# A gated mix of linear attention and eight experts on one core: the queries' sums by head move from TensorE to ScalarE and VectorE, a Silu moves behind a copy, and tiles are resized

## The chip, the cores and the metric

The kernel runs on one core of a Trainium2 chip. The core has five engines with a queue of instructions each: TensorE (PE in the profile, with its weight loads as PEld), VectorE (DVE), ScalarE (ACT), GpSimd (POOL) and SyncE (SP). Each engine takes its instructions strictly in the order in which the program emits them, and waits on semaphores where an operand isn't ready or a buffer isn't free. SP, POOL and ACT also issue DMAs. The metric is the device time of one execution in microseconds; lower is better.

## The reference

`x` has 2048 rows (tokens) of 512. Two branches are computed from it and mixed row by row:

```
qkv = x @ wqkv                                  # 32 heads of 16
phi(t) = where(t > 0, t + 1, exp(t)) + 1e-6;    pq, pk = phi(q), phi(k)
kv  = sum_s pk v^T   (per head, 16 x 16);       z = sum_s pk   (per head, 16)
o   = (pq kv) / (pq . z + 1e-6);                a = o @ wo
b   = sum_e  softmax(x @ w_gate)_e * (silu(x @ w1[e]) @ w2[e])     # all 8 experts, F = 1792
out = g * a + (1 - g) * b,    g = sigmoid(x . gate_w)
```

The divisor `pq . z` is the "sum by head" of the title: for each token and each of the 32 heads, a sum over the head's 16 features of `phi(q) * z`.

## The kernel before

**Number format.** Every fp32 operand of a large product is split into a high part in TensorE's fast fp32 format and a low remainder, and a product is three matmuls (`mm3`, lines 60 to 62: high by high, high by low, low by high). The high part is a ScalarE copy (`act_copy`, line 65), the low part a VectorE subtraction.

**Stages.** `keys` (the first 103 us) loads x, computes phi(k), the router's logits and the gate's (`g_proj`, matmuls of line 459, two passes of 256 and 266 columns from the weights `gw`), and accumulates `ys` = phi(k) with x over 16 blocks of 128 tokens (`y_acc`: moving operand `pkh`, stationary operand `xt`). For the first 12 blocks `xt` lies in the pool `w1p`, for the last four in the pool `att`; `pkh` always lies in `att`. `pks` sums phi(k) by DMA. Then `experts` runs one long loop over the step `u`. The branch b and the branch a use the same machinery: the attention is the ninth "expert", whose first weights are wq and whose second weights are wo folded with kv.

**The loop.** The first layer goes by groups `g` (a pair of 128-feature blocks of one expert, for one half of the tokens), and a group takes seven steps `k` = 0 to 6 of `up`, one product of six matmuls each, in a seven-product scheme on 2 x 2 blocks. The products share four PSUM banks: two under the tag "a", one "b", one "c". ScalarE and VectorE read a bank between two products that accumulate in it, so TensorE waits where such a read is late. In step 3 `hidden(g, 0, 0, ...)` applies Silu to bank b; in step 4 `act_copy(sn[g, 2], bank a)` copies bank a, which product 5 of step 6 goes on accumulating in; step 5 adds bank c on VectorE (line 698), step 6 adds bank a on VectorE (line 704), and product 6 (step 1 of the next group, `a<-t6h` in the early groups) accumulates in that bank once more.
From step u = 58 on, each step also holds a tick `n = u - 58` of the second layer (`tick`, six matmuls `p<-ho,w`), with results taken out of PSUM in `evict`. A step with its tick lasts some 2.7 us. `other()` emits the preparatory work of a step ahead of its matmuls: weights of the next groups (`prep`), high and low parts of the hidden values (`high`, `low_h`), block differences (`differ`) and the queries.
The order of groups is: the two of the attention for half 0, the experts of half 0, four experts of half 1, the attention for half 1, the other four experts. So the first expert's first group is g = 2, and its first Silu (step u = 17) is the first use of that function; a table load on ScalarE stands ahead of it in the trace.

**The queries.** phi(q) is written to DRAM (`pqd`) in four pieces i = 0 to 3 of 512 features by 512 tokens. While the parts of `m.beside` (experts 0, 1, 4 and 5 of half 1) run, one piece each is loaded (at s = -3, s being the tick within the part), gets the constant 1e-6, is divided by its heads' sums and multiplied by the gate g, and is written back:

- `queries_first`, s = 0 to 3: `act_copy(..., bias=EPS)` on ScalarE, one of the four feature blocks each tick
- `queries_last`, s = 3: four products `Q.z` by `Q.d` on TensorE (line 1040, 32 columns of weights, plain fp32, which the trace shows as 8 matmul records), into a bank of tag "a"
- s = 4: a ScalarE copy of that bank to `r`; SP loads the gate, broadcast to 128 partitions
- s = 5 to 8: four reciprocals of 128 columns; s = 9: the product with the gate, and four POOL DMAs to DRAM (`rd`)
- s = 10 and 15: POOL DMAs read `rd` back so that a head's value stands on its 16 partitions (line 1006); s = 15 to 18: four VectorE products (line 1030) and the write to `pqd`

`normaliser` makes `Q.z` at u = 7: z by 32 tiny matmul records (line 943) against `ones`, masked with `maskh` on VectorE, and parked in DRAM (`zcd`).

**The end.** The last part is the attention of half 1, two groups (`A[1]`). In its product P5, `evict` adds the banks to the sums already loaded (`sums`, tile `tl`, line 843), two VectorE adds for each `sub`; then `columns(2)` and `turn_last` transpose some of the sums on TensorE (lines 1083, 1104), and `last_rows` accumulates the last product onto them.

**Tile addresses.** All tiles of the pools `xpool`, `w1p`, `hq` and `w2p` have sizes that are multiples of 256 bytes for each partition, and lie 128 bytes past a multiple of 256. In `att`, the second weight tile g1 has 8576 bytes (33 and a half times 256), so what comes after it in that pool (the raw x tiles, `hl` and `xe` with `pkh` and the split x) lies at a multiple of 256.

Of the kernel before, what the change touches and what calls it, by code (L numbers as in the profile page):

```python
# [16 lines left out]
P = 128  # L17
# [3 lines left out]
E = 8  # L21
# [23 lines left out]
def gated_mix_kernel(ctx: ExitStack, tc: tile.TileContext, xT, x, wk, wv, wqkv_q, wo, wm, out):  # L45
# [59 lines left out]
    m.zcd = dram.tile([P, KT * NH], F32, name="zcd")  # L105
    m.rd = dram.tile([2, 2, NH, TB], F32, name="rd")

# [218 lines left out]
def keys(m):  # L326
# [34 lines left out]
    maskh = m.maskh = misc.tile([P, KT, NH], F32, name="maskh")  # L361
# [33 lines left out]
    v.memset(f32(zero), 0.0)  # L395
# [52 lines left out]
    def bands(t):  # L448
        if t == 5:
            band(mask.rearrange("p (b e) -> p b e", e=DH), [[-DH, P // DH], [0, DH]], 1)  # L450
        elif t == 6:
            band(maskh, [[P, KT], [-DH, NH]], 1)

    pk = {}

# [130 lines left out]
def experts(m, misc):  # L586
# [58 lines left out]
    def touch():  # L645
        b = ps_tile("b", "b")
        o, at = ops[0][0]
        nc.tensor.matmul(b, o[:, 0, at:at + P], XO[0][0][0][:, 0], start=True, stop=True)

    def up(g, k, mid, other):
        old = g > 0
        new = g < NG
        if k == 0:
            other()
            if old:
                hidden(g - 1, 1, 1, sn[g - 1, 3], sn[g - 1, 3])
            if new:
                bank[g, "a"] = ps_tile(f"a{g}", "a")  # L660
                product(g, 0, bank[g, "a"], True)
            mid()
            if new:

                bank[g, "b"] = ps_tile(f"b{g}", "b")
                act_copy(bank[g, "b"], bank[g, "a"])
        elif k == 1:
            other()
            if old:
                product(g - 1, 6, bank[g - 1, "a"], False)  # L670
            mid()
            if old:
                hidden(g - 1, 1, 0, r_tile(f"s4_{g - 1}"), bank[g - 1, "a"])
        elif k == 2:
            other()
            if new:
                bank[g, "c"] = ps_tile(f"c{g}", "c")
                product(g, 1, bank[g, "c"], True)
            mid()
            if new:  # L680
                sn[g, 3] = r_tile(f"s3_{g}")
                act_copy(sn[g, 3], bank[g, "c"])
        elif k == 3:
            other()
            product(g, 2, bank[g, "b"], False)
            mid()
            hidden(g, 0, 0, r_tile(f"s1_{g}"), bank[g, "b"])
        elif k == 4:
            other()
            product(g, 3, bank[g, "a"], False)  # L690
            mid()
            sn[g, 2] = r_tile(f"s2_{g}")
            act_copy(sn[g, 2], bank[g, "a"])
        elif k == 5:
            other()
            product(g, 4, bank[g, "c"], False)
            mid()
            v.tensor_add(sn[g, 2], bank[g, "c"], sn[g, 2])  # L698
        else:
            other()  # L700
            hidden(g, 0, 1, sn[g, 2], sn[g, 2])
            product(g, 5, bank[g, "a"], False)
            mid()
            v.tensor_add(sn[g, 3], bank[g, "a"], sn[g, 3])  # L704
# [125 lines left out]
    def evict(part, prod, sub):  # L830
        b = pb[bank_of(part, prod), sub]
        e = f"{part.h}_{part.e}{sub}"

        own = part is m.parts[-2]
        if part is m.A[1]:

            if prod == "P1":
                own_bank(sub)
                return

            for r, j in {"P7": [(1, 1)], "P2": [(0, 0)], "P4": [(1, 0)], "P6": [(1, 0)], "P5": [(0, 1), (1, 1)]}[prod]:
                s = sums[1, r * 2 + sub, j]
                v.tensor_add(s, b, s)
# [93 lines left out]


    def normaliser():
        ps = ps_tile("z", "dn")[:, :KT * NH]  # L940
        for c in range(KT):
            for a in range(QT):
                nc.tensor.matmul(ps[a * SQ:(a + 1) * SQ, c * NH:(c + 1) * NH],
                                 m.pks[:, c * P + a * SQ:c * P + (a + 1) * SQ], m.ones, start=(c == 0), stop=True,
                                 skip_group_check=True)
        zf = r_tile("zf")[:, :KT * NH].rearrange("p (c f) -> p c f", c=KT)
        v.scalar_tensor_tensor(zf, ps.rearrange("p (c f) -> p c f", c=KT), S * EPS, m.maskh, op0=ALU.add, op1=ALU.mult)
        nc.sync.dma_start(m.zcd, zf.rearrange("p c f -> p (c f)"))

    def gates(step):  # L950
        g = m.lg[:, :, :E]
# [36 lines left out]

    Q = SimpleNamespace()

    def queries_load(i):
        if i % 2 == 0:
            az = m.raw_tile(f"az{i}")
            Q.z = az[:, :KT * NH].rearrange("p (c f) -> p c f", c=KT)
            Q.by = [az[:, KT * NH + c * TB:KT * NH + (c + 1) * TB] for c in (0, 1, 2, 0)]
            nc.sync.dma_start(az[:, :KT * NH], m.zcd)
# [4 lines left out]
    def queries_first(i, s):  # L1001
        h, j = divmod(i, 2)

        def spread(c):
            heads = m.rd[h, j, c * P // DH:(c + 1) * P // DH]
            nc.gpsimd.dma_start(Q.by[c], heads[:, None, :].to_broadcast([P // DH, DH, TB]))

        if 0 <= s < KT:
            act_copy(Q.d[:, s], Q.d[:, s], bias=EPS)
        elif s == 4:  # L1010
            r = Q.r = out_tile(f"r{i}")
            Q.gate = out_tile(f"rg{i}")
            at = (2 * h + j) * TB
            nc.sync.dma_start(Q.gate, m.wgtd[E:E + 1, at:at + TB].to_broadcast([P, TB]))
            act_copy(r, Q.ps, bias=EPS)
        if 5 <= s < 9:
            r = Q.r[:, (s - 5) * P:(s - 4) * P]
            v.reciprocal(r, r)
        elif s == 9:
            v.tensor_mul(Q.r, Q.r, Q.gate)  # L1020
            for c in range(KT):
                n = P // DH
                at = c * (NH + n)
                nc.gpsimd.dma_start(m.rd[h, j, c * n:(c + 1) * n], Q.r[at:at + n])
        elif s == 10:
            for c in range(KT - 1):
                spread(c)
        if 15 <= s < 15 + KT:
            d = Q.d[:, s - 15]
            v.tensor_mul(d, d, Q.by[s - 15])  # L1030
            nc.sync.dma_start(m.pqd[h, j, s - 15], d)
            if s == 15:
                spread(KT - 1)

    def queries_last(i, s):

        if s == KT - 1:
            Q.ps = ps_tile(f"dn{i}", "a")
            for c in range(KT):
                nc.tensor.matmul(Q.ps[c * NH:(c + 1) * NH, :], Q.z[:, c], Q.d[:, c], start=True, stop=True)  # L1040


    def load_query(part, i):
# [104 lines left out]
    for u in range(LAG + NTICK):  # L1148
# [2 lines left out]
        g, k = divmod(u, 7)  # L1151


        query = [(i, n - part.t0) for i, part in enumerate(m.beside) if -3 <= n - part.t0 < 20]

        def mid():
            if n >= 0:
                tick(n)
            for i, s in query:
                queries_last(i, s)  # L1160


        def spare(i, name):
# [7 lines left out]
        def other():  # L1171
# [16 lines left out]
            for i, s in query:  # L1188
                if s == -3:
                    queries_load(i)  # L1190
                queries_first(i, s)
            q, s = divmod(u - 7 * WP, 21)
            if 0 <= q < 2 and s == 0:
                m.load_wp(q)
# [100 lines left out]
```

## Time and profile before

| | us |
|---|---|
| median of 3 runs | 2328.27 (2327.76, 2328.27, 2330.57) |
| profiled execution | 2327.1 |
| its span, first to last instruction | 2325.1 |
| TensorE busy | 2317.9 |
| VectorE busy | 1808.4 |
| ScalarE busy | 1400.4 |
| GpSimd busy | 171.2 |

The granted TensorE clock is full throughout. A line of the page's groups names the line of the kernel, the engine, the operation, the tile written and the tiles read, then the count, the busy time in us and the mean duration in ns. In a timeline a row is the start in us, the duration in us, the engine, the line and the tiles. Matmuls are pipelined, so one that shows 0.39 us lets the next start 0.23 us later: a cost on TensorE is read from start to start, not from durations.

### The profile page before, as it was taken

How to read it: one execution, taken by the hardware profiler on the slowest of the kernel's cores; microseconds unless marked ns; L12 is line 12 of the kernel's file. 1: busy time of each engine (PE TensorE's matmuls, PEld its weight loads, DVE VectorE, ACT ScalarE, POOL GpSimd, SP SyncE). 2: the span in 40 equal slices, each digit the busy share in tenths (PEclk: the TensorE clock that was granted, in tenths of full speed). 3: DMA queues.
4: the chain of work that ended last, by engine and by line, in shares of the span. 5: the costliest groups of instructions: out<-in, count | busy, mean ns of one | idle time of the engine just before them, and what ended most of it. 6: DMA issues, size and time to landing. Idle time of an engine off the chain costs nothing.

```text
span 2325.1 us, 31697 instructions
## 1 busy us (share of the span) xinstructions
PE 2317.9 (100%) x10582; PEld 1919.7 (83%) x10582; DVE 1808.4 (78%) x3088; ACT 1400.4 (60%) x2641; POOL 171.2 (7%) x241
## 2 busy tenths in 40 slices
PE   9999999999999999999999999999999999999999
PEld 8888888888888888888888888888888888888887
DVE  6798888888888878888677768776777776777777
ACT  6687656666666666666555555555565555555553
POOL 1101000000000000000001001000011100100101
PEclk9999999999999999999999999999999999999999
DMA  7898888988889798888846556665556646666568
GB/s 233 235 305 293 269 278 255 286 261 264 266 271 282 250 290 259 264 271 258 290 138 178 166 182 172 178 187 143 162 174 181 201 152 185 182 164 175 161 220 223
DMA packets 325620, 517.54 MB, mean 223 GB/s; under 512 B 51328, under 2 KB 220560, under 8 KB 325072
## 3 DMA queue, kind: packets, MB, share of 16 engines
q1 hardware_dynamic: 294720, 463.91, 60.5%
q0 software_dynamic: 26080, 50.69, 11.9%
q8 instruction: 83, 1.36, 0.2%
q10 hardware_dynamic: 4656, 0.92, 0.2%
q14 instruction: 81, 0.66, 0.1%
HBM read 347.75 MB, written 163.45 MB: 220 GB/s over the span
## 4 chain that ended last, share of the span: by engine, by line
PE 99%; ACT 0%; issue 0%; DVE 0%
PE p L60 16%; PE p L62 16%; PE p L61 16%; PE a L60 9%; PE a L61 9%; PE a L62 9%; PE c L60 4%; PE c L62 4%; PE c L61 4%; PE b L60 2%; PE b L62 2%; PE b L61 2%; PE g L459 2%; PE y L60 1%; PE y L62 1%; PE y L61 1%
## 5 line engine op out<-in xcount | busy, mean ns | idle before, releaser
L60 PE MATMUL p<-ho,w 128*128 128x512 f32 x1602 | 623.2, 389 | 0.0
L61 PE MATMUL p<-ho,w 128*128 128x512 f32 x1602 | 623.2, 389 | 0.0
L62 PE MATMUL p<-ho,w 128*128 128x512 f32 x1602 | 623.2, 389 | 0.0
L768 DVE TENSOR_TENSOR ho<-s,ho 128x512 fp32r<-128x512 f32 x784 | 536.7, 685 | 41.0 <-ACT ho L65 38.3
L65 ACT ACTIVATE ho<-s 128x512 fp32r<-128x512 f32 x784 | 481.4, 621 | 16.0 <-PE p L62 10.8
L62 PEld LDWEIGHTS p<-ho,w 128*128 128x128 f32 x1602 | 300.6, 188 | 62.7
L60 PEld LDWEIGHTS p<-ho,w 128*128 128x128 f32 x1602 | 300.7, 188 | 62.3
L61 PEld LDWEIGHTS p<-ho,w 128*128 128x128 f32 x1602 | 300.7, 188 | 62.3
L65 ACT ACTIVATE o<-rs 128x512 fp32r<-128x512 f32 x224 | 129.2, 577 | 205.7 <-PE c L62 114.0
L65 ACT ACTIVATE o<-rm 128x512 fp32r<-128x512 f32 x240 | 138.4, 577 | 142.1 <-PE a L62 68.4
L698 DVE TENSOR_TENSOR s<-c,s 128x512 f32<-128x512 f32 x116 | 80.1, 690 | 156.9 <-PE c L62 150.6
L65 ACT ACTIVATE ws<-rm 128x256 fp32r<-128x256 f32 (+1 forms) x204 | 115.0, 572 | 53.1 <-DMA w2stash<-ws 48.7
L627 ACT ACTIVATE s<-s 128x512 f32<-128x512 f32 x224 | 138.4, 618 | 6.2 <-DVE s L704 3.7
L704 DVE TENSOR_TENSOR s<-a,s 128x512 f32<-128x512 f32 x116 | 80.1, 690 | 63.2 <-PE a L62 63.2
L627 ACT ACTIVATE s<-b 128x512 f32<-128x512 f32 x112 | 67.0, 598 | 102.9 <-PE b L62 91.0
L65 ACT ACTIVATE s<-a 128x512 f32<-128x512 f32 x116 | 69.3, 597 | 92.1 <-PE a L62 92.1
L207 DVE TENSOR_TENSOR o<-rm,o 128x512 fp32r<-128x512 f32 x180 | 123.0, 683 | 1.3 <-ACT o L65 1.2
L221 DVE TENSOR_TENSOR ws<-rm,ws 128x512 fp32r<-128x512 f32 x155 | 106.1, 685 | 21.2 <-ACT ws L65 19.4
L207 DVE TENSOR_TENSOR o<-rs,o 128x512 fp32r<-128x512 f32 x168 | 114.5, 682 | 8.5 <-ACT o L65 8.5
L65 ACT ACTIVATE b<-a 128x512 f32<-128x512 f32 x116 | 67.2, 579 | 64.2 <-PE a L62 64.2
L65 ACT ACTIVATE s<-c 128x512 f32<-128x512 f32 x116 | 69.0, 595 | 26.3 <-PE c L62 26.3
L827 POOL DMA_DIRECT2D acct<-c x30 | 26.3, 876 | 693.0 <-DVE c L821 526.4
(331 smaller groups left out, 4521.1 us busy)
## 6 DMA issues: line engine op xcount, KB each, us to landing
w<-w2stash SPq DMA_DIRECT2D x403, 512.0 KB, 4.2
w2stash<-ws SPq DMA_DIRECT2D x359, 256.0 KB, 4.6
rm<-wm SPq DMA_DIRECT2D x228, 256.0 KB, 5.2
rs<-wm SPq DMA_DIRECT2D x108, 256.0 KB, 4.2
wb<-wgtd SPq DMA_DIRECT2D x16, 512.0 KB, 4.8
acct<-c POOLq DMA_DIRECT2D x30, 256.0 KB, 6.2
acct<-d POOLq DMA_DIRECT2D x30, 256.0 KB, 5.2
acct<-k POOLq DMA_DIRECT2D x30, 256.0 KB, 5.3
```

The source lines that it names most:

```text
L60: nc.tensor.matmul(ps, wh, xh, start=start, stop=False, skip_group_check=True)
L61: nc.tensor.matmul(ps, wh, xl, start=False, stop=False, skip_group_check=True)
L62: nc.tensor.matmul(ps, wlo, xh, start=False, stop=stop, skip_group_check=True)
L65: nc.scalar.activation(dst, src, AF.Copy, scale=scale, bias=bias)
L207: v.tensor_sub(two(o, 1), src, f32(two(o, 0)))
L221: v.tensor_sub(two(w, 1), src, f32(two(w, 0)))
L459: nc.tensor.matmul(ps, xk((0, 0, 1)[j], tb, k, tt * P, (tt + 1) * P), gw[g][:, (0, 1, 0)[j], k, :], start=(k == 0 and j == 0), stop=(k == ...
L627: nc.scalar.activation(dst, src, AF.Silu)
L698: v.tensor_add(sn[g, 2], bank[g, "c"], sn[g, 2])
L704: v.tensor_add(sn[g, 3], bank[g, "a"], sn[g, 3])
L768: v.tensor_sub(h[1], s, f32(h[0]))
L827: nc.gpsimd.dma_start(m.acct[part.h, j, dt], s, accum_op=ALU.add)
```

## The change

1. **Sums by head.** The four small products on TensorE are gone, with the DRAM round trips `zcd` and `rd`. `normaliser` now uses two columns of `ones` instead of 32 and keeps z, one value for each feature, in a small SBUF tile `m.z`; `maskh` is gone. For each piece, over 22 ticks instead of 19: for each of the four feature blocks c, ScalarE adds 1e-6 as before and writes a second copy scaled by `m.z` (a value per partition); VectorE transposes that copy in squares of 32 and, a tick later, reduces groups of 16 columns to a head's sum. Then one addition and one reciprocal of 128 columns (s = 12), one product with the gate (s = 13), and for each c a transpose whose input repeats each value 16 times (back to features on partitions) and, a tick later, the product with the block and its write. The gate is loaded by four POOL DMAs at s = -3, as 32 x 16 elements of 4 bytes each.
2. **Phase.** g1 takes 320 columns for each row block instead of 266 (10240 bytes), so the tiles of `att` after it lie 128 bytes past a multiple of 256, like those of the other pools.
3. **First Silu.** For group EXP0 (g = 2) alone, `hidden(g, 0, 0, ...)` is emitted in step 4 behind the copy of bank a, instead of in step 3.
4. **End.** In P5 of the last part, `sub` 0 adds its two sums in the other order.

```diff
+    EXP0 = m.parts[0].gs[0]
...
-            hidden(g, 0, 0, r_tile(f"s1_{g}"), bank[g, "b"])
+            if g != EXP0:
+                hidden(g, 0, 0, r_tile(f"s1_{g}"), bank[g, "b"])
         elif k == 4:
...
             act_copy(sn[g, 2], bank[g, "a"])
+            if g == EXP0:
+                hidden(g, 0, 0, r_tile(f"s1_{g}"), bank[g, "b"])
...
-    gw = [att.tile([P, 2048 + 96 * i], F32R, name=f"g{i}")[:, :2 * KT * G[i]] for i in range(2)]
-    gw = [g.rearrange("p (c k f) -> p c k f", c=2, k=KT) for g in gw]
+    gw = [att.tile([P, 2 * KT * w], F32R, name=f"g{i}") for i, w in enumerate((256, 320))]
+    gw = [g.rearrange("p (c k f) -> p c k f", c=2, k=KT)[:, :, :, :n] for g, n in zip(gw, G)]
...
+            last = [(1, 1), (0, 1)][::1 - 2 * sub]
+            for r, j in {"P7": [(1, 1)], "P2": [(0, 0)], "P4": [(1, 0)], "P6": [(1, 0)], "P5": last}[prod]:
...
+    QS = 3 * KT + 2 + 2 * KT
...
+            *Q.t, Q.sq, rest = (az[:, c * TB:(c + 1) * TB] for c in range(KT))
+            Q.r, Q.gate = rest[:, :P], rest[:, P:P + TB // SQ]
...
+        gate = m.wgtd[E, i * TB:(i + 1) * TB].rearrange("(b i) -> i b", i=SQ)
+        for a in range(QT):
+            nc.gpsimd.dma_start(Q.gate[a * SQ:(a + 1) * SQ], gate)
+
+    def queries(i, s):
...
+        if 0 <= s < 3 * KT:
+            c, step = divmod(s, 3)
+            if step == 0:
+                act_copy(Q.d[:, c], Q.d[:, c], bias=EPS)
+                nc.scalar.activation(Q.t[c % 2], Q.d[:, c], AF.Copy, scale=m.z[:, c:c + 1])
+            elif step == 1:
+                v.transpose(Q.sq, Q.t[c % 2])
+            else:
+                v.tensor_reduce(heads(c), Q.sq.rearrange("p (n f) -> p n f", f=DH), axis=AX.X, op=ALU.add)
+        elif s == 3 * KT:
+            v.tensor_scalar(Q.r, Q.r, EPS, None, op0=ALU.add)
+            v.reciprocal(Q.r, Q.r)
+        elif s == 3 * KT + 1:
+            r = Q.r.rearrange("p (c b h) -> p c b h", c=KT, h=SQ // DH)
+            v.tensor_mul(r, r, Q.gate[:, None, :, None].to_broadcast([P, KT, TB // SQ, SQ // DH]))
+        elif s < QS:
+            c, step = divmod(s - 3 * KT - 2, 2)
+            if step == 0:
+                v.transpose(Q.t[c % 2], heads(c)[:, :, None].to_broadcast([P, SQ, DH]))
+            else:
+                d = Q.d[:, c]
+                v.tensor_mul(d, d, Q.t[c % 2])
+                nc.sync.dma_start(m.pqd[h, j, c], d)
```

More of the change, by code (lines that the diff above doesn't have):

```diff
@@ L104, in gated_mix_kernel @@
     m.wpd = [dram.tile([P, D], F32, name=f"wpd{c}") for c in range(KT)]
-    m.zcd = dram.tile([P, KT * NH], F32, name="zcd")
-    m.rd = dram.tile([2, 2, NH, TB], F32, name="rd")
     X = [[SimpleNamespace(e=e, h=h, n=NPAIR) for e in range(E)] for h in range(2)]
@@ L360, in keys @@
     mask = m.mask = misc.tile([P, P], F32, name="mask")
-    maskh = m.maskh = misc.tile([P, KT, NH], F32, name="maskh")
     pks = m.pks = misc.tile([P, D], F32, name="pks")
@@ L450, in bands @@
             band(mask.rearrange("p (b e) -> p b e", e=DH), [[-DH, P // DH], [0, DH]], 1)
-        elif t == 6:
-            band(maskh, [[P, KT], [-DH, NH]], 1)
     pk = {}
@@ L839, in evict @@
                 return
-            for r, j in {"P7": [(1, 1)], "P2": [(0, 0)], "P4": [(1, 0)], "P6": [(1, 0)], "P5": [(0, 1), (1, 1)]}[prod]:
+            last = [(1, 1), (0, 1)][::1 - 2 * sub]
+            for r, j in {"P7": [(1, 1)], "P2": [(0, 0)], "P4": [(1, 0)], "P6": [(1, 0)], "P5": last}[prod]:
                 s = sums[1, r * 2 + sub, j]
@@ L939, in normaliser @@
     def normaliser():
-        ps = ps_tile("z", "dn")[:, :KT * NH]
+        ps = ps_tile("z", "dn")[:, :2 * KT]
         for c in range(KT):
             for a in range(QT):
[L943 to L948, printed above, removed]
+                nc.tensor.matmul(ps[a * SQ:(a + 1) * SQ, 2 * c:2 * c + 2],
+                                 m.pks[:, c * P + a * SQ:c * P + (a + 1) * SQ], m.ones[:, :2], start=(c == 0),
+                                 stop=True, skip_group_check=True)
+        m.z = hp.tile([P, 2 * SQ], F32, name="z", tag="z", bufs=1)
+        v.tensor_scalar(m.z[:, :KT], ps.rearrange("p (c f) -> p c f", f=2)[:, :, 0], S * EPS, None, op0=ALU.add)
     def gates(step):
@@ L993, in queries_load @@
             az = m.raw_tile(f"az{i}")
-            Q.z = az[:, :KT * NH].rearrange("p (c f) -> p c f", c=KT)
-            Q.by = [az[:, KT * NH + c * TB:KT * NH + (c + 1) * TB] for c in (0, 1, 2, 0)]
-            nc.sync.dma_start(az[:, :KT * NH], m.zcd)
+            *Q.t, Q.sq, rest = (az[:, c * TB:(c + 1) * TB] for c in range(KT))
+            Q.r, Q.gate = rest[:, :P], rest[:, P:P + TB // SQ]
         Q.d = m.raw_tile(f"pq{i}").rearrange("p (c t) -> p c t", c=KT)
@@ L999, in queries_load @@
             nc.sync.dma_start(Q.d[:, c], m.pqd[i // 2, i % 2, c])
-    def queries_first(i, s):
+        gate = m.wgtd[E, i * TB:(i + 1) * TB].rearrange("(b i) -> i b", i=SQ)
+        for a in range(QT):
+            nc.gpsimd.dma_start(Q.gate[a * SQ:(a + 1) * SQ], gate)
+    def queries(i, s):
         h, j = divmod(i, 2)
[L1004 to L1040, printed above, removed]
+        def heads(c):
+            return Q.r[:, c * SQ:(c + 1) * SQ]
+        if 0 <= s < 3 * KT:
[21 more added lines that the diff above has]
+                nc.sync.dma_start(m.pqd[h, j, c], d)
@@ L1151, in experts @@
         g, k = divmod(u, 7)
-        query = [(i, n - part.t0) for i, part in enumerate(m.beside) if -3 <= n - part.t0 < 20]
+        query = [(i, n - part.t0) for i, part in enumerate(m.beside) if -3 <= n - part.t0 < QS]
         def mid():
@@ L1158, in mid @@
                 tick(n)
-            for i, s in query:
-                queries_last(i, s)
         def spare(i, name):
@@ L1190, in other @@
                     queries_load(i)
-                queries_first(i, s)
+                if s >= 0:
+                    queries(i, s)
             q, s = divmod(u - 7 * WP, 21)
```

## The prediction

> **What bounds the kernel now.** I read, in this order: the page's busy times and chain, TensorE's own waits, then timelines around the places that the change touches.
>
> ```profile
> span 2325.1 us, 31697 instructions
> ...
> PE 2317.9 (100%) x10582; PEld 1919.7 (83%) x10582; DVE 1808.4 (78%) x3088; ACT 1400.4 (60%) x2641; POOL 171.2 (7%) x241
> ...
> PE 99%; ACT 0%; issue 0%; DVE 0%
> ```
>
> ```profile
> PE idle L523 <- DVE zero L395: 1.5, 1, 1.5
> PE a L60 <- ACT s L65: 0.7, 1, 0.7
> ```
>
> TensorE is the chain from end to end, and in the whole span it waits by name twice. So what leaves TensorE's queue leaves the time one for one, and added work on VectorE or ScalarE costs nothing until it makes TensorE wait. All that counts below is measured on TensorE from start to start.
>
> **Sums by head off TensorE: -6.6 us.** The first of the four places:
>
> ```profile
> 1256.73 0.39 PE L62 MATMUL p<-ho,w 128*128 128x512 f32 x1
> 1257.05 1.52 PE L1040 MATMUL dn<-pq,az 128*32 128x512 f32 x8
> 1258.50 0.50 PE L60 MATMUL a<-n5h,o 128*128 128x512 f32 x1
> 1258.83 0.40 PE L61 MATMUL a<-n5l,o 128*128 128x512 f32 x1
> ...
> L1040 PE MATMUL dn<-pq,az x32: 592/605/617, 1257.0 to 1967.5; 128*32 128x512 f32 x32
> ```
>
> From the start of the last ordinary matmul ahead (1256.73) to that of the second behind (1258.83) pass 2.10 us; without the eight records it would be two ordinary steps of 0.227 (from the last pair of the rows on phase, below), 0.45. That is 1.65 us a piece, changeover included (the matmul behind takes 0.33 to the next start instead of 0.23), and 32 records make four pieces: 6.6 us. The end bounds are 6.6 and, if each piece comes back as a wait, 0. I take 6.6, since the bank that the products took from tag "a" and the ScalarE copy of it go too.
>
> **What takes their place, on VectorE and ScalarE: 0.** The fullest 22 ticks, today:
>
> ```profile
> 1248.00:1308.00 60.00, 60.00 (x267) 48.53 (x266) 46.51 (x81) 34.46 (x65) 4.60 (x9) 1.00 0.60 185
> ...
> L1018 DVE RECIPROCAL r<-r x16: 943/945/947, 1262.0 to 1980.1; 128x128 f32<-128x128 f32 x16
> ...
> L1064 DVE STREAM_TRANSPOSE row<-acc x8: 701/704/705, 2038.5 to 2171.7; 128x512 f32<-128x512 f32 x8
> ...
> L966 DVE TENSOR_REDUCE gates<-gates x1: 228/228/228, 187.1 to 187.1; 128x16 f32<-128x128 f32 x1
> ...
> L969 DVE TENSOR_TENSOR gates<-gates x1: 284/284/284, 189.4 to 189.4; 128x128 f32<-128x128 f32 x1
> ```
>
> VectorE is busy 46.5 of 60 us. Gone are three of four reciprocals (2.8). Added are four plain transposes (0.70 each, 2.8), two small operations of 128 columns (0.3 each by line 969, 0.6), and eight instructions of unknown price p: four reductions of 512 columns to 32, and four transposes that read each value 16 times. That makes 47.1 + 8p. Below, p is 0.23 (a reduction of a quarter of the input); above, 3.8 (four times the reciprocal, the slowest row for an element). I take 0.70, the transpose row, nearest in form and size: 52.7 of 60, so VectorE keeps up. Over 60 it comes at p = 1.6. ScalarE gains four scaled copies and loses one copy, some 1.9 us at 0.62 each (row at 126.36 below), on 34.5 of 60.
>
> The tightest hand-over in these ticks is where P2 ends and P4 takes its bank, now beside the block transposes:
>
> ```profile
> 1305.36 0.68 DVE L821 TENSOR_TENSOR c<-p,wb 128x512 f32<-128x512 f32 x1
> ...
> 1306.08 0.60 ACT L65 ACTIVATE p<-k 128x512 f32<-128x512 f32 x1 [1.07 <-DVE c L821]
> ...
> 1308.95 0.39 PE L60 MATMUL p<-ho,w 128*128 128x512 f32 x1
> ```
>
> The ScalarE copy is done at 1306.68, TensorE needs the bank at 1308.95: 2.27 us to spare, 1.57 with one more instruction of 0.70 ahead. Behind a VectorE transpose that waits for its scaled copy stand the subtractions for the hidden values and the bank adds; the copy is emitted a whole tick (2.7 us) ahead, so I cost that wait at nothing.
>
> The Trainium skill, "VectorE: DVE Perf Modes", section "Rules for kernel authors", warns of `tensor_reduce` on a hot path as the slowest VectorE operation. The rows disagree at 128 columns: the reduction took 228 ns, the product beside it 284. By the page p would lie nearer its upper end, which is the last rival below; by the rows it stays cheap.
>
> **DMAs: 0.** Off SP go `zcd` and the gate's broadcast, off POOL 32 issues of `rd`; POOL gets 16 issues of 512 elements of 4 bytes, ahead of the sums of the part that ends.
>
> ```profile
> q0 software_dynamic: 26080, 50.69, 11.9%
> ...
> q10 hardware_dynamic: 4656, 0.92, 0.2%
> ```
>
> The page (packets, MB, share of 16 engines) gives 16 ns for one packet of q10 (0.2% of 16 engines' span, 198 bytes on average) and 170 ns for one of q0. A piece's 2048 elements over 16 engines then hold each for 2 to 22 us, spread among the others' packets, and the gate is needed 16 ticks (43 us) after the issue. POOL is 7% busy; what queues behind it, the sums into DRAM, has no reader for a part.
>
> **First Silu behind the copy: +0.75 us, a loss.** Today's rows of ScalarE, TensorE and VectorE:
>
> ```profile
> 124.58 1.28 ACT L627 ACT_TABLE_LOAD   x1
> 125.87 0.60 ACT L627 ACTIVATE s<-b 128x512 f32<-128x512 f32 x1
> 126.36 0.62 ACT L65 ACTIVATE o<-rm 128x512 fp32r<-128x512 f32 x1
> 126.88 0.59 ACT L65 ACTIVATE s<-a 128x512 f32<-128x512 f32 x1
> 127.36 0.63 ACT L65 ACTIVATE wx<-rm 128x512 fp32r<-128x512 f32 x1
> ```
>
> ```profile
> 126.47 0.39 PE L62 MATMUL c<-x11h,o 128*128 128x512 f32 x1
> 127.53 0.50 PE L60 MATMUL a<-t5h,o 128*128 128x512 f32 x1 [0.67 <-ACT s L65]
> ...
> 130.38 0.39 PE L60 MATMUL a<-t6h,o 128*128 128x512 f32 x1
> ```
>
> ```profile
> 125.40 0.69 DVE L257 TENSOR_TENSOR rm<-rm 128x512 f32<-128x512 f32 x1
> ...
> 128.66 0.68 DVE L221 TENSOR_TENSOR wx<-rm,wx 128x512 fp32r<-128x512 f32 x1
> 129.26 0.68 DVE L704 TENSOR_TENSOR s<-a,s 128x512 f32<-128x512 f32 x1
> ```
>
> TensorE stands 0.83 us (127.53 - 126.47 - 0.23) for the copy of bank a, which stands behind table load and Silu. With both behind it, the copy `o<-rm` ahead is held by VectorE's line 257 (ends 126.09), so it runs 126.13 on, the copy of bank a 126.65 to 127.24, and TensorE starts at 127.30: only 0.23 won. Then the table load (to 128.54) and the Silu stand ahead of `wx<-rm`, which starts near 129.04 and ends 129.67 instead of 127.99. VectorE's line 221 waits for it, and behind line 221 in VectorE's queue stands line 704: 130.30 to 130.98. Product 6 (`a<-t6h`) needs that; it would be due at 130.15 and starts near 131.03, 0.88 late, plus 0.1 for a second changeover as behind line 1040. So -0.23 + 0.88 + 0.1 = +0.75. Bounds: -0.94 (whole wait and changeover gone, nothing late behind) and +1.3 (the 1.28 of the load uncovered).
>
> **Phase: -0.6 us.** The same 12 matmuls of `y_acc` for a block whose `xt` lies in `w1p`, at the other phase than `pkh` (first pair of rows), and for the last block, both in `att` (second pair):
>
> ```profile
> 74.08 0.40 PE L60 MATMUL y<-pkh,xt 128*128 128x512 f32 x1
> ...
> 76.86 0.40 PE L459 MATMUL g<-g,x30h 128*128 128x256 f32 x2
> ...
> 93.86 0.39 PE L60 MATMUL y<-pkh,xt 128*128 128x512 f32 x1
> ...
> 96.59 0.39 PE L648 MATMUL b<-x00h,o 128*128 128x512 f32 x1
> ```
>
> 2.78 against 2.73 us: 0.05 a block, 12 blocks, 0.6. Bounds: 0.8 (were it all 16 blocks) and 0 if something else in that stage is the cause; for the first loads into the moved x tiles I take 0, within 0.2 either way.
>
> The Trainium skill, "SBUF — State Buffer", section "SBUF: two separate sides", says that PE's port never waits on anyone, so where operands lie would not matter and this term would be 0. The rows disagree by 4 ns a matmul; as the cause is unproved, the page's case is a rival.
>
> **End: -0.2 us. Normaliser: 0.**
>
> ```profile
> 2314.04 2.65 DVE L843 TENSOR_TENSOR tl<-p,tl 128x512 f32<-128x512 f32 x4
> ...
> 2314.97 0.39 PE L62 MATMUL p<-ho,w 128*128 128x512 f32 x1
> ...
> 2315.39 0.66 PE L1083 MATMUL oc<-ident,tl 128*128 128x128 f32 x4
> ...
> 108.32 0.46 PE L943 MATMUL z<-ones,pks 128*32 128x32 f32 x32
> ```
>
> Line 1083 needs the second of four adds (end 2315.37); swapped it has the first (2314.70) and starts at 2315.20, 0.19 sooner. The third add, for line 1104, ends 2316.03, and its reader comes past 2316.1, so the gain is kept. The 32 records of line 943 stay 32: at most their 0.46 could go.
>
> **Sum.** -6.6 + 0.75 - 0.6 - 0.2 = -6.65 us. Against the profiled 2327.1 (span 2325.1 and 2.0 around it) that is 2320.5; the median of the runs lies 1.2 above the profiled execution, so 2321.6.
>
> **The rivals.**
> - *The Silu's move helps.* The whole 0.94 goes and line 704 isn't late: 1.7 better, 2319.9. For it: one ScalarE operation fewer ahead of the wait. Against: line 704 starts right behind line 221 in the rows, so whatever holds the one holds the other.
> - *Phase is nothing*: 2322.2, still faster.
> - *Part comes back.* Scaled copy and bank reads meet on ScalarE, VectorE stands for a transpose, and a bank add behind it is late, 0.5 to 1.2 us a piece: 2323.6 to 2326.4, about no change. For it: the same coupling costs in the Silu's rows. Against: a tick between copy and transpose.
> - *VectorE becomes the bound in the queries' ticks: slower.* Over p = 1.6 it can't finish 22 ticks' work in 60 us; the excess is 8p - 12.9 a piece. Four times that cancels the gain at p = 1.8 and makes it slower by 0.2% at p = 2.0; at 3.8 it is 17.5 a piece, 2392. For it: a transpose with a repeated input has no row. Against: plain transpose and reduction are cheap.
>
> **How the numbers follow.** 0.2% (4.7 us here) is about what a measurement can tell from no change. Forecast 0.64, Silu helps 0.10, phase nothing 0.08: all faster by over 0.2%, 0.82. Part comes back 0.11, taken as within 0.2%. VectorE bound 0.07, slower. The forecast's own range is 2320.3 to 2322.8. The range 2319.0 to 2324.3 takes in the first two rivals and the lower end of the third.
>
> **What would show it.** Right: no line 1040, from one ordinary matmul to the next 0.23 us there; in the 22 ticks VectorE near 53 of 60 and no wait of TensorE; around 127 us a wait of some 0.6 for bank a and a second near 130 for line 704; 12 `y` matmuls in 2.73 throughout. Wrong: TensorE waiting for VectorE between 1248 and 1308 or in the three later places, reductions or repeated transposes over 1.6 us, or a wait for weights `w` beside the gate's loads.

## The result and the profile after

The changed kernel takes 2320.61 us (median of 10 runs, 2319.96 to 2326.39) against 2327.82 us (10 runs, 2327.23 to 2330.57) for the kernel before on the same chip: a ratio of 0.9971 with a 95% interval of 0.9962 to 0.9981, faster by 7.2 us. Two of the ten executions took some 5 us more than the rest (2325.58 and 2326.39), and two of ten in the second set (run 1) 4 and 7 us more; no trace of one of them was kept. The forecast was 2321.6 with a range of 2319.0 to 2324.3. The profiled execution took 2320.65 us, with a span of 2318.9: 6.2 us less span than before.

The page of the changed kernel (span; busy time of each engine; shares of the chain that ended last):

```profile
span 2318.9 us, 31635 instructions
...
PE 2310.3 (100%) x10550; PEld 1918.3 (83%) x10550; DVE 1826.5 (79%) x3128; ACT 1407.7 (61%) x2653; POOL 161.0 (7%) x222
...
PE 99%; ACT 0%; issue 0%; DVE 0%; ACTq 0%
```

TensorE has 32 matmuls fewer and is still the chain from end to end. VectorE has 18 us more to do, and TensorE's span does not show them. TensorE's waits by name in the changed kernel (line, what was waited for, us in all, times, longest):

```profile
PE idle L518 <- DVE zero L392: 1.5, 1, 1.5
PE kv L914 <- issue: 1.3, 1, 1.3
PE a L60 <- DVE s L705: 0.7, 1, 0.7
PE a L60 <- ACT s L65: 0.5, 1, 0.5
```

Before there were the first and the last. The third is the second wait that the forecast put near 130 us. The second was not foreseen. The places where the change acts, in the timeline of TensorE of the changed kernel (start, duration, line, tiles):

```profile
73.27 0.39 PE L60 MATMUL y<-pkh,xt 128*128 128x512 f32 x1
...
75.99 0.40 PE L454 MATMUL g<-g,x30h 128*128 128x256 f32 x2
...
102.72 1.27 PE L914 MATMUL kv<-yT,wv 128*32 128x32 f32 x118
105.29 0.31 PE L914 MATMUL kv<-yT,wv 128*32 128x32 f32 x10 [1.30 <-issue]
...
126.49 0.39 PE L62 MATMUL c<-x11h,o 128*128 128x512 f32 x1
127.38 0.50 PE L60 MATMUL a<-t5h,o 128*128 128x512 f32 x1 [0.49 <-ACT s L65]
...
131.13 0.50 PE L60 MATMUL a<-t6h,o 128*128 128x512 f32 x1 [0.74 <-DVE s L705]
...
1257.66 0.39 PE L62 MATMUL p<-ho,w 128*128 128x512 f32 x1
1257.89 0.39 PE L60 MATMUL a<-n5h,o 128*128 128x512 f32 x1
...
2309.25 0.39 PE L62 MATMUL p<-ho,w 128*128 128x512 f32 x1
2309.48 0.60 PE L1077 MATMUL oc<-ident,tl 128*128 128x128 f32 x4
```

Read downwards: the 12 `y` matmuls take 2.72 us (2.78 before); the products `kv` stop once for 1.30 us; the first expert waits twice; where the sums by head stood, one ordinary matmul follows the other by 0.23 us; at the end line 1077 starts 0.23 us after the matmul ahead of it (0.42 before).

The two executions can be laid over each other, matmul by matmul (without the 32 that went), and the difference of the start times read off at each stage. The "ledger" below means this difference of two traces, in us; negative is earlier.

| stretch | forecast | ledger, changed minus before |
|---|---|---|
| up to the first `kv` product (104 us) | -0.6 (phase) | -0.98 |
| inside the 128 `kv` products | none | +1.18 |
| from there to the first expert | 0 | -0.17 |
| around the first Silu (125 to 131 us) | +0.75 | +0.84 |
| four places of the sums by head | -6.6 | -6.69 |
| end, line 1077 | -0.2 | -0.18 |
| last matmul to the end of the span | 0 | -0.30 |
| whole span | -6.65 | -6.13 |

The rows leave 0.17 us of small shifts in other places. The medians differ by 7.2 us and the profiled executions by 6.45 (2327.1 and 2320.65); executions of one kernel scatter by more than the 0.75 between these two. The forecast had set the median 1.2 us above the profiled execution. With ten runs of the kernel before that distance is 0.7, and for the changed kernel it is nothing (2320.61 and 2320.65).

### The profile page after: what moved, and what is told of

Read it like the earlier page. It is cut to its first block, busy times and chain, and to the rows that moved or that the text cites. A ratio compares the mean times of both kernels' runs of the same rounds, so it can differ in the third digit from the quotient of the medians.

```text
span 2318.9 us, 31635 instructions
## 1 busy us (share of the span) xinstructions
PE 2310.3 (100%) x10550; PEld 1918.3 (83%) x10550; DVE 1826.5 (79%) x3128; ACT 1407.7 (61%) x2653; POOL 161.0 (7%) x222
## 3 DMA queue, kind: packets, MB, share of 16 engines
q1 hardware_dynamic: 293712, 462.66, 59.9%
## 4 chain that ended last, share of the span: by engine, by line
PE 99%; ACT 0%; issue 0%; DVE 0%; ACTq 0%
PE p L61 16%; PE p L62 16%; PE p L60 16%; PE a L60 9%; PE a L61 9%; PE a L62 9%; PE c L60 5%; PE c L61 4%; PE c L62 4%; PE b L62 2%; PE b L61 2%; PE b L60 2%; PE g L454 2%; PE y L60 1%; PE y L61 1%; PE y L62 1%
```

## The experiments

Each kernel changes the kernel after, or the kernel before where that is said. Times of one set of runs share the runs of the kernel before.

**1. The changed kernel once more.** The question was whether the unforeseen wait inside `kv` belongs to the program.

> The changed kernel once more, unaltered. Theory A (the 1.3 us that TensorE stands inside the kv products near 104 us, with no wait named, belongs to the program): the same wait of 1.2 to 1.4 us again. Theory B (it falls differently in every execution): another length there, 0 to 0.4 as before the change, and a span 1.0 to 1.2 us shorter. Both: about 2320.6 by the clock outside, ratio to before 0.997.

Measured: 2320.86 us (10 runs), ratio 0.9972 (0.9963 to 0.9982), with a `kv` wait of 1.0 us instead of 1.3, between what the two theories had said. By itself this looked like a property of the program; run 8 shows that its length is not.

**2. The Silu back in step 3.** The rest of the change stays.

```
-            if g != EXP0:
-                hidden(g, 0, 0, r_tile(f"s1_{g}"), bank[g, "b"])
+            hidden(g, 0, 0, r_tile(f"s1_{g}"), bank[g, "b"])
 ...
-            if g == EXP0:
-                hidden(g, 0, 0, r_tile(f"s1_{g}"), bank[g, "b"])
```

> The changed kernel with the first Silu back in step 3, ahead of the copy of bank a; all else as changed. Theory (the move costs): one wait for bank a near 126.5 us of 0.8 instead of 0.66, no wait for the VectorE add near 130; 0.84 us off the time from one matmul ahead to the matmuls behind, so about 2319.8. Rival (the move helps, and the wait near 130 comes from something else): the wait near 130 stays at 0.9 and the time rises by 0.2.

Measured: 2319.5 us (5 runs, 2319.24 to 2320.71), ratio 0.9965 (0.9952 to 0.9977), against 2320.86 for the changed kernel in the same set. TensorE's waits in the work itself, with the Silu back:

```profile
PE a L60 <- ACT s L65: 0.7, 1, 0.7
PE kv L910 <- issue: 0.6, 1, 0.6
```

The wait for line 705's sum is gone, so the rival fell. Against the changed kernel the ledger at this place gives +0.17 (first wait longer), -0.90 (second wait gone) and -0.11 (its changeover gone): -0.84. The Silu's move is a loss of 0.84 us, as forecast in place and nearly in size. The mechanism stands in the rows of ScalarE in the changed kernel:

```profile
126.21 0.63 ACT L65 ACTIVATE o<-rm 128x512 fp32r<-128x512 f32 x1 [1.62 <-DVE rm L255]
126.74 0.58 ACT L65 ACTIVATE s<-a 128x512 f32<-128x512 f32 x1
127.34 1.28 ACT L622 ACT_TABLE_LOAD   x1
128.63 0.60 ACT L622 ACTIVATE s<-b 128x512 f32<-128x512 f32 x1
129.13 0.62 ACT L65 ACTIVATE wx<-rm 128x512 fp32r<-128x512 f32 x1
```

and in those of VectorE in the same kernel:

```profile
129.78 0.69 DVE L219 TENSOR_TENSOR wx<-rm,wx 128x512 fp32r<-128x512 f32 x1 [1.02 <-ACT wx L65]
130.40 0.68 DVE L705 TENSOR_TENSOR s<-a,s 128x512 f32<-128x512 f32 x1
```

ScalarE now idles 1.62 us for `rm`, in which load and Silu stood before; load and Silu push `wx<-rm` to 129.13; line 219 waits for it, and line 705 behind line 219 feeds the matmul at 131.13.

**3. The table loaded early, the Silu still behind the copy.** In step 3 a Silu of one column, whose result is overwritten, loads the table in ScalarE's idle time.

```
-            if g != EXP0:
+            if g == EXP0:
+                m.s1 = r_tile(f"s1_{g}")
+                nc.scalar.activation(m.s1[:, :1], m.ident[:, :1], AF.Silu)
+            else:
                 hidden(g, 0, 0, r_tile(f"s1_{g}"), bank[g, "b"])
```

> The changed kernel with one added Silu of a single column in step 3, whose only purpose is to load the table there, in the 1.6 us that ScalarE then stands for VectorE; the first full Silu stays behind the copy. Theory (what stands ahead of wx on ScalarE makes VectorE's bank add late): table load near 124.6, wx 1.3 us earlier, the wait of 0.9 for the add gone, the wait of 0.66 for the copy of bank a stays (it is set by VectorE's line 255): 1.0 off, about 2319.6. Rival (VectorE's own backlog makes the add late): wait near 130 stays over 0.5.

Measured: 2320.07 us (8 runs), ratio 0.9969 (0.9959 to 0.998). ScalarE with the early load:

```profile
124.75 1.28 ACT L687 ACT_TABLE_LOAD   x1
126.04 0.20 ACT L687 ACTIVATE s<-ident 128x1 f32<-128x1 f32 x1
126.35 0.63 ACT L65 ACTIVATE o<-rm 128x512 fp32r<-128x512 f32 x1
126.89 0.58 ACT L65 ACTIVATE s<-a 128x512 f32<-128x512 f32 x1
...
127.84 0.63 ACT L65 ACTIVATE wx<-rm 128x512 fp32r<-128x512 f32 x1
```

`wx<-rm` runs 1.29 us sooner and the second wait is gone. The first wait stays at 0.5 us: the copy of bank a stands behind `o<-rm`, which waits for VectorE, and not behind Silu or table. So the copy ahead is the limit of what the move can win at the first wait, as the forecast had it. (This execution has no wait at `kv`, but one of 1.3 us for the sums `pks`; see run 6.)

**4. Early table, and the product and copy of bank a put ahead of step 4's other work.** Relative to run 3:

```
-            other()
+            if g != EXP0:
+                other()
             product(g, 3, bank[g, "a"], False)
             mid()
 ...
+            if g == EXP0:
+                other()
```

> As the run with the early table load, and in step 4 of that group the product and the copy of bank a are emitted ahead of the step's other work, so the copy doesn't stand behind the copy that VectorE's line 255 holds. Theory: no wait for bank a near 126.5 (0 to 0.1), but VectorE has no gap from 124 on, so its bank add still ends near 130.0 and the product that needs it, now due near 129.5, waits 0.5: in all 0.9 to 1.1 off the changed kernel, about 2319.5. Rival (ScalarE alone sets both waits): both gone, 1.7 off, about 2318.9.

Measured: 2320.13 us (5 runs), ratio 0.9965 (0.9953 to 0.9978). The one wait that is left there:

```profile
130.35 0.50 PE L60 MATMUL a<-t6h,o 128*128 128x512 f32 x1 [0.39 <-DVE s L711]
```

The first wait is gone (-0.75 in the ledger against the changed kernel, changeover included), and of the second a half remains (-0.35): -1.1 in all. The rival expectation, that both vanish, fell, for the reason that the theory gave: VectorE runs without a gap from 124.42 on, so its line 711 starts at 129.61, no sooner than the same add in run 3 (129.43, in an execution that is 0.18 us ahead there). TensorE, without its first wait, now comes to it earlier. Medians of runs 2 to 4 differ by 0.6 us, which they can't tell apart; only the ledger does.

**5. The sums by head alone.** Phase, Silu and end as before.

```
-    gw = [att.tile([P, 2 * KT * w], F32R, name=f"g{i}") for i, w in enumerate((256, 320))]
-    gw = [g.rearrange("p (c k f) -> p c k f", c=2, k=KT)[:, :, :, :n] for g, n in zip(gw, G)]
+    gw = [att.tile([P, 2048 + 96 * i], F32R, name=f"g{i}")[:, :2 * KT * G[i]] for i in range(2)]
+    gw = [g.rearrange("p (c k f) -> p c k f", c=2, k=KT) for g in gw]
 ...
-            last = [(1, 1), (0, 1)][::1 - 2 * sub]
+            last = [(0, 1), (1, 1)]
```

and the Silu as in run 2.

> The kernel before with the sums by head moved to ScalarE and VectorE alone; phase, first Silu and the order at the end as before. Theory: 4 pieces of 1.65 us are all of the gain, 6.6 us off the span, about 2321.2; no wait of TensorE in the queries' ticks; the y products 2.78 us a block as before. Rival (the phase or the end carries more of it): under 6 us.

Measured: 2320.99 us (8 runs), ratio 0.9971 (0.9961 to 0.9982). The ledger is -6.69 us over the four places and -6.19 at the end of the span. So the first part is all of the gain that can be measured; phase, Silu and end, with the waits that vary, together come to nothing that shows. The rival fell.

**6. The phase alone.** The kernel before, with the tile of `g1` made wider, which also widens the distance between its rows.

```
-    gw = [att.tile([P, 2048 + 96 * i], F32R, name=f"g{i}")[:, :2 * KT * G[i]] for i in range(2)]
-    gw = [g.rearrange("p (c k f) -> p c k f", c=2, k=KT) for g in gw]
+    gw = [att.tile([P, 2 * KT * w], F32R, name=f"g{i}") for i, w in enumerate((256, 320))]
+    gw = [g.rearrange("p (c k f) -> p c k f", c=2, k=KT)[:, :, :, :n] for g, n in zip(gw, G)]
```

> The kernel before with the resized g1 alone (320 columns a row block). Theory: the first layer's keys stage loses 1.0 us up to the kv products (0.7 of it in the y products of blocks 0 to 11, at 2.73 us a block), nothing else moves. Rival (the stage got shorter for another reason, such as the freed mask): under 0.3.

Measured in one execution: 2333.01 us, slower than before (2328.24). The 144 `y` matmuls of the 12 blocks concerned are 0.227 apart, as in the changed kernel, and the ledger is -0.86 up to `kv` (1.0 was expected). Then comes a wait (TensorE's timeline of this kernel):

```profile
111.72 0.66 PE L943 MATMUL z<-ones,pks 128*32 128x32 f32 x32 [4.28 <-DMA pks<-pk]
```

The products `z` need `pks`, which 15 DMAs add up one after the other, most of them waiting for the landing of the one ahead. Here their median time to landing is 5.3 us and the last was issued at 107.7, in the changed kernel 4.0 us and 98.4 (the groups of tile `pks`, first and last start at the end of the line; this kernel, then the changed one):

```profile
L479 POOL DMA_DIRECT2D pks<-pk x15: 862/862/911, 22.6 to 107.7; - x15
```

```profile
L474 POOL DMA_DIRECT2D pks<-pk x15: 844/852/908, 22.4 to 98.4; - x15
```

**7. The same phase by 128 and by 64 bytes of room behind `g1`, the distance between its rows kept.** Both change the kernel before: `96 * i` becomes `128 * i` (tiles of the pools at one phase) or `112 * i` (64 bytes off).

```
-    gw = [att.tile([P, 2048 + 96 * i], ...
+    gw = [att.tile([P, 2048 + 128 * i], ...
```

> The kernel before with 128 bytes of padding behind g1 and its row blocks still 266 columns apart: only the phase of the tiles behind it moves. Theory (the phase of stationary against moving tile counts): y blocks 0 to 11 at 2.73 us as with the resized g1; the g products of 266 columns keep their uneven steps. Rival (the pitch of g1's rows counts): y stays at 2.78.

> The kernel before with 64 bytes of padding behind g1, so that the tiles behind it lie 64 bytes from the phase of the other pools, instead of 128 before and 0 in the change. Theory (any difference in phase costs): y blocks 0 to 11 between 2.75 and 2.80 us. Rival (only the half of 256 does): 2.73.

Measured in one execution each: 2329.86 and 2328.36 us (before: 2328.24). The first also waits 1.2 us for a copy of weights near 7 us, and both wait 0.7 us for a load of `w` near 1139 us.

Of the 12 blocks of `y` matmuls concerned, most take 2.763 us with 128 bytes (two take 2.720), and all take 2.80 with 64. In the kernel before and in run 5, which has its layout, most take 2.782, in the changed kernel all 2.72. So the time of these matmuls goes with the layout, but one phase brings most blocks only a third of the way (0.020 of 0.063 us). Neither expectation for 128 bytes (2.73 and 2.78) came, and with 64 bytes the blocks are slower than before. The `g` products between the blocks take 0.2 us more in all with 128 bytes. From the 100th matmul (near 17 us) to the first `kv` product the ledger is then -0.1 us for the one phase, against -0.9 in run 6 and in the changed kernel.

Run 6 brings the full effect, but it differs from run 7 in two ways: the rows of `g1` are wider apart, and the tiles behind it move by 1664 bytes instead of 128. Which of the two counts, and why, no run here tells.

**8. Runs 6 and 7 (128 bytes) again, timed.**

> The kernel before with the resized g1 alone, timed. In the one look its keys stage was 0.86 us shorter up to the kv products, and then the products of the normaliser waited 4.3 us for the last of the 16 sums into pks. Theory (that wait belongs to one execution; the chain of sums ends anywhere between 102 and 112 us): median 0.3 to 1.0 below before, profile with a wait under 1.5 us there. Rival (the shorter stage always runs into the chain of sums): median 3 to 6 above before, the wait of over 3 us again.

> The kernel before with the padding alone, timed. In the one look y blocks 0 to 11 were at 2.73 us a block, but the first products waited 1.2 us for a copy of weights and a product of the second layer 0.7 us for a load. Theory (those two belong to one execution): median 0 to 0.8 below before. Rival (moving the first x tiles makes the start longer): the wait of 1.2 us near 7 us again, median 0.5 to 1.5 above.

Measured: 2327.89 us (11 runs, 2325.97 to 2333.19), ratio 1.0001 (0.9992 to 1.001); and 2328.12 us (11 runs), ratio 1.0 (0.9991 to 1.0009). The wait of run 6 is not there in this execution of the same kernel; in its place stands the other one (TensorE's timeline, run 6's kernel, second execution):

```profile
102.90 1.28 PE L912 MATMUL kv<-yT,wv 128*32 128x32 f32 x118
105.75 0.31 PE L912 MATMUL kv<-yT,wv 128*32 128x32 f32 x10 [1.57 <-issue]
108.96 0.46 PE L943 MATMUL z<-ones,pks 128*32 128x32 f32 x32
```

One program, two executions: once 4.28 us for `pks` and none at `kv`, once 1.57 at `kv` and none for `pks`. So both waits vary from execution to execution, by up to 4.3 us, and the gain of run 6's layout (0.86 up to `kv` in the first execution, 0.81 in the second) can't be seen behind them. The expectation that the wait of run 6 would always come fell, and one of 0.3 to 1.0 us gained isn't borne out by the medians either (0.2). With 128 bytes the wait near 7 us is 0.5 this time, and the one for `w` is not there.

**9. VectorE's new work twice and three times.** Four transposes, four reductions and four transposes with a repeated input are issued two (three) times a piece, with the same result.

```
-                v.transpose(Q.sq, Q.t[c % 2])
+                for _ in range(2):
+                    v.transpose(Q.sq, Q.t[c % 2])
```

and likewise for lines 1020 and 1030.

> The changed kernel with each of the twelve transposes and reductions of a piece issued twice, the same result. VectorE busy in the 60 us from 1248 goes from 51.5 to 58.7. Theory (VectorE's time in the queries' ticks is free up to 60 of 60): TensorE waits under 0.5 us in all there, time as changed (2320.6). Rival (hand-overs inside a tick bind earlier): waits of 0.5 to 2 us a piece.

> The same three times: 65.9 us of VectorE work for 60 us of ticks. Theory: over the bound, TensorE waits for VectorE, 2 to 6 us a piece (part of the excess runs into the emptier ticks behind), 8 to 24 in all, 2329 to 2345. Rival (there is more slack, from work ahead): under 1 us a piece.

First the prices in the changed kernel (tile `az`: durations in ns, least, middle, most; first and last start):

```profile
L1016 ACT ACTIVATE az<-pq,z x16: 722/725/726, 1248.3 to 1977.0; 128x512 f32<-128x512 f32 x16
L1018 DVE STREAM_TRANSPOSE az<-az x16: 701/711/715, 1250.2 to 1978.6; 128x512 f32<-128x512 f32 x16
L1020 DVE TENSOR_REDUCE az<-az x16: 677/679/682, 1252.1 to 1982.6; 128x32 f32<-128x512 f32 x16
L1030 DVE STREAM_TRANSPOSE az<-az x16: 699/705/708, 1285.8 to 2009.1; 128x512 f32<-128x512 f32 x16
L1033 DVE TENSOR_TENSOR pq<-pq,az x16: 678/686/689, 1288.8 to 2011.8; 128x512 f32<-128x512 f32 x16
```

and the 60 us from 1248 (window, then TensorE, weight loads, VectorE, ScalarE, POOL busy, granted clock) in the changed kernel, with the work twice, and with it three times:

```profile
1248.00:1308.00 60.00, 60.00 (x267) 49.67 (x266) 51.49 (x92) 37.14 (x70) 3.50 (x5) 1.00 0.51 161
```

```profile
1248.00:1308.00 60.00, 60.00 (x266) 49.73 (x265) 55.98 (x98) 35.92 (x67) 4.44 (x6) 1.00 0.49 149
```

```profile
1248.00:1308.00 60.00, 56.09 (x240) 45.76 (x239) 58.06 (x101) 32.68 (x60) 2.89 (x5) 0.97 0.40 128
```

Measured: 2326.66 and 2350.99 us, one run each (before: 2328.65). By the sum, twelve instructions more of 0.70 make 51.5 + 8.4 = 59.9 of 60 for VectorE; twice twelve make 68.3, over by 8.3 a piece or 33 in four. The ledger from 1250 us on gives +1.7 us against the changed kernel with the work twice (0.42 a piece) and +31.2 with it three times. The rest of the 6.0 us by which the span grew with the work twice is lost ahead of these ticks: 3.9 by 131 us (most of it a `pks` wait of 2.0 us with slow matmuls behind it) and 0.5 near 1140 us.

With the work twice VectorE is not yet full: 55.98 of 60 in the row above, 57.0 from 1253 to 1313 (this execution is 4.4 us late there). The 0.42 a piece is lost at one place, the hand-over from P2 to P4 that the forecast called the tightest. In the changed kernel the ScalarE copy starts at 1305.94 and ends at 1306.54, and TensorE takes the bank at 1308.21, 1.67 us later (1.57 forecast). With the work twice two transposes stand ahead of VectorE's add, and the slack is gone (VectorE, ScalarE, TensorE):

```profile
1310.13 1.45 DVE L1033 STREAM_TRANSPOSE az<-az 128x512 f32<-128x512 f32 x2
1311.51 0.65 DVE L822 TENSOR_TENSOR c<-p,wb 128x512 f32<-128x512 f32 x1
...
1312.19 0.60 ACT L65 ACTIVATE p<-k 128x512 f32<-128x512 f32 x1 [2.40 <-DVE c L822]
...
1312.35 0.39 PE L62 MATMUL b<-n2h,o 128*128 128x512 f32 x1
1312.85 0.50 PE L60 MATMUL p<-ho,w 128*128 128x512 f32 x1
```

TensorE's waits with the work three times:

```profile
PE a L60 <- DVE s L705: 19.0, 9, 3.1
PE p L60 <- ACT p L65: 3.2, 2, 1.6
```

For twice, the theory (under 0.5 us in all) and the rival (0.5 to 2 us a piece) both missed: it measured 1.7 in all, at a place of the rival's kind. The expectation of 2 to 6 us a piece for three times was too low: it measured 7.8. There the sum is well over 60 and VectorE is the bound (58.06 us busy while TensorE works 56.09), as the last rival of the forecast had it. The first loss comes before the sum is used up, where one hand-over inside a tick has no slack left.

## Why the prediction was right

**Sums by head.** Right: -6.69 for -6.6. Nothing takes the place of the 32 matmuls; TensorE has no wait by name in the queries' ticks, and run 5 shows this part alone to carry the result.

**VectorE as cover.** Right, and for the reason given: p was put at 0.70 by the transpose row and measured 0.68 (reduction) and 0.705 (repeated transpose); 52.7 was forecast and 51.5 is measured. Run 9 shows that the cover was real and nearly used up by as much again. The forecast set against the row a rule of the Trainium skill, "VectorE: DVE Perf Modes", section "Rules for kernel authors", which calls `tensor_reduce` the slowest VectorE operation. The rows don't bear it out: the reduction took 679 ns, the product of as many columns on line 1033 took 686. ScalarE came to 37.1 where 34.5 + 1.9 = 36.4 was forecast: the scaled copy takes 725 ns, not 620. The Trainium skill, "ScalarE: Activation LUTs", section "What ACT_TABLE_LOAD costs", gives about 93 ns for an operand with one value per partition; here the scaled copy takes 107 ns more than the copy of the same size ahead of it (618), which is near that.

**DMAs and normaliser.** Right at 0: no wait for `w` or for the gate is in the changed kernel's waits, the gate's loads land 5.8 us after their issue (median; 7.6 at most) where 43 are there, and the burst of 32 `z` products costs the same within 0.03 us.

**First Silu.** Right in place, sign and size: the second matmul waits at 131.13 (131.03 forecast), the loss is 0.84 (0.75 forecast). Runs 2 to 4 separate its parts: what costs is the table load ahead of `wx<-rm`; what limits the gain is the copy `o<-rm` ahead and, once that is out of the way, VectorE's own queue (run 4).

**Phase.** The gain is there, and was put too low; the reason given for it isn't borne out. Up to `kv` the ledger is -0.98 for -0.6: 776 ns of excess go from the `y` matmuls, some 0.13 us from steps of the `g` products and beside them, and the rest is scatter of the first 17 us. All nine executions with run 6's `g1` reach the first `kv` product at 102.4 to 103.1 us, the two with the layout of before (before and run 5) at 103.7 and 103.8. But one phase alone, run 7 with 128 bytes, gains 0.1 in that stage, in both of its executions. The forecast read the last block only. The block ahead of it, whose two tiles also lie in `att`, takes 2.76 us in the kernel before:

```profile
91.10 0.40 PE L60 MATMUL y<-pkh,xt 128*128 128x512 f32 x1
...
93.86 0.39 PE L60 MATMUL y<-pkh,xt 128*128 128x512 f32 x1
```

The two ahead of that take 2.76 and 2.75. So two tiles at one phase did not mean 2.73, and that the term came out near its size is in part luck. Against the Trainium skill's "SBUF — State Buffer", section "SBUF: two separate sides", by which TensorE never waits at its port, the rows of this place and run 7 show steps that depend on where the operands lie; that contention is the cause is not shown.

**What was not foreseen.** The waits at `kv` and at `z`. In the changed kernel +1.18 us at `kv` takes back the phase's gain. The span's -6.13 lies 0.5 from the forecast's -6.65 because an error of -0.4 in the phase, of +0.1 at the Silu, this +1.2, and -0.3 at the end of the span partly cancel. The profiled time, 2320.65 for 2320.5, is nearer still by the same luck; the median lies 1.0 below its forecast because the 1.2 us above the profiled execution were not there. The forecast came out for its main term, not for its small ones.

**What stays open.** The `kv` wait always comes behind the 118th of the 128 products and is 0 to 1.6 us long; no semaphore ends it. Late instructions are the likely cause: in all 14 traces the 119th product starts 1.2 to 1.5 us after the end of a 16 KB packet of an instruction queue, and TensorE waits where that is later than its 118th product allows. In the changed kernel the packet ends at 104.00 and the product starts at 105.29; in run 8 it is 104.36 and 105.75, in run 6, without a wait, 102.82 and 104.18. No run moves the packet, so the cause is not shown. It was not tried either to take the `z` products away from the end of the chain of `pks` sums.

## What to carry to other kernels

Where TensorE bounds the whole span, a matmul taken off it is worth its step from start to start, and work put on VectorE is free until its sum in that stage comes close to the stage's length, or until a hand-over inside a tick has used up its slack: add it up by stage, with durations of the rows, and look at the tightest hand-over. Before an operation is moved past another on an in-order engine, look at what it now stands ahead of, and at who waits for that: here a table load moved out of an idle stretch cost more than the copy it made room for. A gain of under a microsecond ahead of a chain of DMAs needs the traces of several executions, since what follows can take it back; the best version seen is the change without the Silu's move (2319.5 us), better than the change by 0.84 us in the ledger and by less than the medians can settle.

## What the runs showed of the hardware

- Matmuls of the same shape step by 0.227 to 0.234 us, depending on the layout of the tiles: a block of 12 takes 2.72 us with run 6's `g1`, 2.78 with the layout of before (most blocks of both executions), 2.76 with 128 bytes of room (most blocks) and 2.80 with 64.
- After a wait of 4.28 us (run 6) the next matmuls start 0.43 us apart, and so they do after one of 3.13 us with the work three times, here in TensorE's timeline of that kernel:

```profile
1284.85 0.80 PE L60 MATMUL a<-n6h,o 128*128 128x512 f32 x1 [3.13 <-DVE s L705]
1285.44 0.63 PE L61 MATMUL a<-n6l,o 128*128 128x512 f32 x1
1285.87 0.63 PE L62 MATMUL a<-n6h,o 128*128 128x512 f32 x1
```

  The granted clock from 1284.85 to 1287.60 is 0.50 in this execution, and so the row of the 60 us has 0.97. Such a wait costs more than itself: by these steps 1.4 us more here, where the sixth matmul is the last slow one, and 2.5 in run 6. The length of the wait alone doesn't decide it: of the four waits of 3.1 us with the work three times, the first and the third were followed by slow steps at once. In the other two pieces the steps stayed at 0.23, and slow ones came only behind the next wait, of 2.1 us. The Trainium skill, "TensorE: Matmul & The Clock Gate", section "Wait — 56ns, not 53.3ns?", gives 426.7 ns for such a step at half clock; these rows agree (0.43).
- A transpose in squares of 32 whose input repeats each value along a row costs 705 ns, as a plain one does (711).
